# When later batches' loads are released, what runs in the head, and who copies the values: a change to a sketched-attention and routed-experts kernel

## The chip, the core and the metric

The kernel runs on one core of a Trainium2 chip. The core has five engines that run their own instruction streams: TensorE (PE; its weight loads are listed as PEld), VectorE (DVE), ScalarE (ACT), GpSimd (POOL) and SyncE (SP), which here only issues transfers. Transfers run on 16 DMA engines that all queues share. The metric is the device time of one execution in microseconds; less is better.

## The reference

The first half is an attention with a polynomial sketch in place of the softmax, on 4 batches, 4 heads, 1088 tokens and a head width of 32. The second sends each of the 4352 tokens, now 128 wide, to two of eight experts.

```python
def phi(x):
    a = np.einsum('rd,bhsd->bhsr', S1, x)          # r = 8
    b = np.einsum('rd,bhsd->bhsr', S2, x)
    return np.einsum('bhsi,bhsj->bhsij', a, b).reshape(*x.shape[:-1], r * r)
q_p, k_p = (phi(q), phi(k))
kv = np.einsum('bhsf,bhsd->bhfd', k_p, v)
z = np.sum(k_p, axis=2)
num = np.einsum('bhsf,bhfd->bhsd', q_p, kv)
den = np.einsum('bhsf,bhf->bhs', q_p, z)[..., None] + 1e-06
x = (num / den), heads side by side               # 4352 x 128
...
noisy_logits = x @ w_gate + np.log1p(np.exp(x @ w_noise)) * noise
top2 = the two largest of each row; top2_w = their softmax
for e in range(8):                                # w1[e]: 128 x 1024, w2[e]: 1024 x 128
    h = np.maximum(x[mask] @ w1[e], 0.0)
    out[mask] += top2_w[mask, k, None] * (h @ w2[e])
```

## The kernel before, in words

**The work.** For each batch, `keys_values` (L635) turns keys and queries by 32x32 blocks on DVE (`turned`, L581), and `features` (L591) makes the sketch of up to four tiles of 128 tokens: PE multiplies by the sketch matrix (L602), `lo` is copied out of PSUM, DVE adds (`ab`, L610) and forms the products (L624, `phk` for keys and `phq` for queries). PE then multiplies products of keys with `vaug`, a copy of the values (L661). `queries` (L698) transposes query products on PE (L709), multiplies (L720) and lets DVE divide. `router` computes gates, picks two experts, and counts on PE where each token goes (`mk`, L926 and L929). GpSimd scatters the weighted token rows to a table in HBM, `xs`, by indirect transfers (L801), each after a memset of `zb` that spaces them (L800).

**Waves and blocks.** The tokens come in five waves: wave 0 is four tiles of batch 0, wave 1 the rest of batch 0, waves 2 to 4 the batches 1 to 3. A `block` (L1022) is 128 or 256 rows of one expert: `xb` is fetched from `xs`, turned into `bT`, multiplied by `w1s` into `hp` (L1087), rectified into `h` (L1095, ACT), multiplied by `w2s` into `acc` (L1102), copied to `y`, and scattered to `pairs`, from which the output is summed. Blocks are counted from 0: 0 to 7 are wave 0's, 8 to 15 wave 1's, 16 to 23 wave 2's, and so on. Blocks 0 to 3 (`DIRECT`) don't go through HBM: PE gathers their rows with a selection matrix `o` made at L1032 (for block 0 two of its four parts on POOL, two on DVE). Blocks 4 to 7 (`QUICK`) are fetched by POOL, all later ones by SP, with four transfers for the rows and one for the indices, and are turned on DVE (L1077). `xb` has five buffers and `bT` three.

**What sets the order.** The order of the instructions on each engine is fixed when the program is built. `Plan` (L38) keeps for each job its engine (or a choice of engines), an estimated cost, a priority, and what it depends on, and takes at each step, of the jobs that could start within 0.3 us of the earliest, the one with the lowest priority number. `LAND`, `KLATE`, `VLATE`, `QLATE` and `MARGIN` are what the planner adds to a transfer's estimated arrival. The estimates only set the order; on the chip each instruction waits for the data it needs, in the order of its engine. `idle` (L1391) fills gaps of PE in the first 28 us with multiplications of zeros (L1407).

**Around the change.** `hold` keeps DVE and PE jobs of batch 1 behind the first router's choice. `later` marks transfers that wait until the fetches of blocks 4 to 7 are complete ("rows first"): the weights of experts 6 and 7, the clears of `xs` from row 512 up, and all loads of batches 2 and 3. All of them are issued by SP (L335), in the order of the plan. `kq` (keys and queries) has two buffers and `vld` (values) one.

Of the kernel before, what the change touches and what calls it, by code (L numbers as in the profile page):

```python
# [174 lines left out]
def kernel(  # L175
# [27 lines left out]
    C = 8  # L203
# [107 lines left out]
    MARGIN = 6.0  # L311
# [6 lines left out]
    def copy(e, o, i):  # L318
        paces.append(A.copy(o, i) if e == "ACT" else V.tensor_copy(o, i))  # L319

    held, hold_dma = [], [False]

    def later(*loads):
        hold_dma[0] = True
        for load in loads:
            load()
        hold_dma[0] = False

    def dma(q, o, i, r, w, prio, size=0, issue=0.45, after=(), done=None, margin=0.0):

        eng = {"SP": Y, "ACT": A, "POOL": G}
        waits = hold_dma[0]

        def emit(e):
            ins = eng[e].dma_start(o(), i())  # L335
            if waits:
                behind(ins, "rows first")
            if done:
                done(ins)
        job = add(q, issue, emit, r=r, w=w, prio=prio, lat=LAND, after=after, size=size)  # L340
        if hold_dma[0]:
            held.append(job)
        job.margin = margin
        return job
# [7 lines left out]
    def load_kq(b, which, prio):  # L352
# [4 lines left out]
                  margin=MARGIN if b > 1 or b and which == "q" else QLATE if which == "q" else KLATE)  # L357
# [223 lines left out]
    def turned(dst, src, c0, c1, prio):  # L581
# [7 lines left out]
        add("DVE", vec(128 * (c1 - c0) if c0 < C else 64), emit, r=[src], w=[(dst, t) for t in range(c0, c1)], prio=prio)  # L589

    def features(jobs, prio, after=(), first=None, early=None):  # L591
# [7 lines left out]
        def emit(e):  # L599
# [12 lines left out]
            in0=x4()[:, :, 0, :], in1=lo.t[rows, 0:n, :], op=ALU.add), r=[ps, lo], w=[ab], prio=prio)  # L612
# [19 lines left out]
    kv_of, behind_first = {}, []  # L632
    behind_gates = []

    def keys_values(b, prio, head=False, after=()):  # L635
        kT, qT, pk, pq, va = new("kT"), new("qT"), new("phk"), new("phq"), new("vaug")
        kld, qld, vld = klds[b], qlds[b], vlds[b]
        for h in range(H):
            add(EV if head else "ACT", either(256) if head else act(256), lambda e, h=h: copy(e, va.t[:, 0:C, h, 0:DH], vld.t[:, h, 0:C, :]),
                r=["ones_v"] + [(vld, l) for l in range(4)], w=[(va, h)], prio=prio + 2.2, after=hold)  # L640
        add("ACT", act(128), lambda e: A.copy(va.t[0:HB, C, :, 0:DH], vld.t[0:HB, :, C, :]),
            r=["ones_v", (vld, 4), (vld, 5)], w=[(va, H)], prio=prio + 2.2, after=hold)
        for i, (c0, c1) in enumerate(((0, 2), (2, 6), (6, 8)) if head else ((0, 4), (4, 8))):
            turned(kT, kld, c0, c1, prio + i)
            features([(kT, t, pk) for t in range(c0, c1)], prio + i + 1, after)
        turned(kT, kld, 8, 9, prio + 1)
# [375 lines left out]
    def block(u, w, e, r, n):  # L1022
# [5 lines left out]
        if u < DIRECT:  # L1028
            oh = new("o")
            for c in range(4):  # L1030
                add(("POOL" if u == 0 and c % 2 else "DVE"), 0.3 if u == 0 and c % 2 else vec(64), lambda e_, c=c: (
# [3 lines left out]
                    r=["place", onehot["pos"], onehot["gm"]], w=[(oh, c)], prio=-900 if u == 0 else 12 + u)  # L1035
# [8 lines left out]
        else:  # L1044
            xb, ix = new("xb"), new("ix")

            def done(ins):
# [3 lines left out]
                wrote(ins, "fetch")  # L1051
            there = routed.get(w, []) + routed.get(w - 1, [])
            rows = xs_e[e, r:r + P * n, :]
            if u < QUICK:
                def done(ins, done=done):
                    done(ins)
                    wrote(ins, "rows first")
                fetch = dma("POOL", lambda: xb.t[:, 0:n, :], lambda: rows.rearrange("(c p) x -> p c x", p=P),
                            there, [xb], -10 + u, size=66e3 * n, issue=0.55, done=done)
                for job in held:  # L1060
# [6 lines left out]
            else:  # L1067
# [3 lines left out]
                for l in range(4):  # L1071
                    dma("SP", lambda l=l: flat()[32 * l:32 * l + 32, :].rearrange("p (g x) -> p g x", x=32),
                        lambda l=l: rows[:, 32 * l:32 * l + 32].rearrange("(g p) x -> p g x", p=32),
                        there, [(xb, l)], -10 + u, size=16e3 * n, issue=0.5, done=done)
                dma("SP", lambda: ix.t[:, 0:n].unsqueeze(2), lambda: rows[:, D:XW].rearrange("(c p) x -> p c x", p=P),
# [269 lines left out]
    load_w(0, 41)  # L1345
    for r in (0, P):
        clear(r, 43)
    load_w(1, 44)
    for e in range(2, E - 2):
        load_w(e, 46 + e)  # L1350
    for r in (2 * P, 3 * P):
# [3 lines left out]
    later(lambda: load_w(E - 2, 53), lambda: load_w(E - 1, 54))  # L1355
    for r in range(4 * P, STATIC, P):
        later(lambda r=r: clear(r, 60 + r / P))
# [4 lines left out]
    keys_values(1, 100)  # L1362
    rest_of_queries(last)
    x, lg, last = queries(0, 4, C + 1, 27)
    router(0, 4, C + 1 - 4, 1, x, lg, 30)
    for b in range(1, B):
        if b > 1:
            later(lambda: load_kq(b, "k", 80 + 100 * b), lambda: load_kq(b, "q", 81 + 100 * b), lambda: load_v(b, 82 + 100 * b))
# [78 lines left out]
```

## Time and profile before

| | us |
|---|---|
| Median of 6 runs | 355.48 |
| Lowest and highest | 353.24 and 356.6 |
| The profiled execution's own time | 353.76 |
| Its span in the trace | 351.8 |
| PE, busy | 338.9 (96%) |
| PE, weight loads | 315.0 (90%) |
| POOL, busy | 233.3 (66%) |
| DVE, busy | 145.7 (41%) |
| ACT, busy | 134.4 (38%) |
| Fillers L1407, 33 of them | 11.1 |

Times in the trace count from the start of the span. A line of the page or of a view names an engine, a line of the code, and the tile that is written and those that are read; the mean duration is that of one instruction; "idle before" is how long the engine had nothing to run, with the instruction that ended the wait. The chain of waits goes back from the last instruction to whatever released it. A transfer appears with the instruction that issues it; when it has landed is seen from what it releases. Instruction records on PE are pipelined, so neighbours overlap by about 0.2 us.

The trace has these stages: until 27.43 the head (loads, batch 0, the first router); until 73.96 blocks 0 to 6 beside batch 1; then block 8 and after beside batches 2 and 3, until about 162; then blocks alone.

### The profile page before, as it was taken

The numbers are of one execution on the slowest core, as the hardware profiler recorded it, in microseconds if no ns is written. First come the engines' busy times: TensorE is split into PE (matmuls) and PEld (weight loads), VectorE is DVE, ScalarE is ACT, GpSimd is POOL, SyncE is SP. The second block draws the span as 40 slices with busy tenths as digits, with TensorE's granted clock in tenths as the row PEclk, the third lists the DMA queues.
The fourth block names the chain that finished last, engine by engine and source line by source line (L and its number), as shares of the span: only waits on it lengthen the run. The fifth ranks groups of instructions, "written<-read, shape, count | busy, mean of one in ns | idle before, by whom it ended". The sixth has DMA issues, their size and how long they took to land.

```text
span 351.8 us, 7486 instructions
## 1 busy us (share of the span) xinstructions
PE 338.9 (96%) x2589; PEld 315.0 (90%) x2590; DVE 145.7 (41%) x547; ACT 134.4 (38%) x301; POOL 233.3 (66%) x385
## 2 busy tenths in 40 slices
PE   8999999969999999999999999999999999999992
PEld 3859999969999999998999999999999999999991
DVE  5879893847966887586301000011012000001401
ACT  2343532534325333333333433343334333434330
POOL 7758569962898989988898988954433443344510
PEclk9999999999999999999999999999999999999997
DMA  8999859933351135512422223553215311115521
GB/s 207 323 345 248 297 141 358 315 70 81 72 169 47 41 69 89 135 47 45 86 60 61 50 48 71 129 156 52 46 31 145 100 39 23 29 25 147 162 81 38
DMA packets 68298, 41.17 MB, mean 117 GB/s; under 512 B 49301, under 2 KB 60438, under 8 KB 68256
## 3 DMA queue, kind: packets, MB, share of 16 engines
q1 hardware_dynamic: 62784, 30.92, 35.4%
q0 software_dynamic: 4736, 9.19, 7.9%
q10 hardware_dynamic: 736, 0.54, 0.6%
q8 instruction: 21, 0.34, 0.4%
q14 instruction: 21, 0.17, 0.2%
HBM read 24.17 MB, written 16.65 MB: 116 GB/s over the span
## 4 chain that ended last, share of the span: by engine, by line
PE 84%; POOL 6%; DVE 5%; DMA 2%; issue 2%; ACT 1%; SPq 0%; POOLq 0%; DVEq 0%
PE acc L1102 33%; PE hp L1087 33%; PE bank L602 4%; POOL xs L801 3%; PE bank L720 3%; PE bank L661 2%; PE bank L709 2%; PE hp L1407 2%; POOL zb L800 1%; PE acc L661 1%; DMA pairs<-y,first_at 1%; PE turn L1038 1%; PE bank L1234 1%; DVE pick L904 1%; DMA xb<-xs 1%
## 5 line engine op out<-in xcount | busy, mean ns | idle before, releaser
L1087 PE MATMUL hp<-bT,w1s 128*128 128x128 f32 (+1 forms) x768 | 148.6, 329 | 3.0 <-DVE bT L1077 3.0
L1102 PEld LDWEIGHTS acc<-w2s,h 128*128 128x128 f32 x1152 | 146.7, 192 | 4.8
L1102 PE MATMUL acc<-w2s,h 128*128 128x128 f32 x1152 | 150.7, 275 | 0.0
L1095 ACT ACTIVATE h<-hp 128x512 f32<-128x512 f32 x144 | 86.0, 597 | 131.8 <-PE hp L1087 131.8
L1087 PEld LDWEIGHTS hp<-bT,w1s 128*128 128x128 f32 x768 | 111.6, 192 | 8.7 <-issue 3.4
L801 POOL DMA_INDIRECT pairs<-y,ix x62 | 62.1, 1002 | 66.1 <-ACT y L319 59.1
L801 POOL DMA_INDIRECT xs<-xg,to x72 | 72.5, 1007 | 13.6 <-issue 9.3
L1077 DVE STREAM_TRANSPOSE bT<-xb 128x256 f32<-128x256 f32 (+1 forms) x40 | 15.5, 388 | 131.6 <-PE hp L1087 124.0
L800 POOL MEMSET zb<- 128x400 bf16 (+1 forms) x142 | 62.8, 443 | 0.2
L319 ACT COPY y<-acc 128x128 f32<-128x128 f32 (+1 forms) x48 | 15.3, 319 | 26.3 <-PE acc L1102 26.3
L1158 DVE TENSOR_TENSOR o<-pr 128x512 f32<-128x512 f32 (+2 forms) x13 | 6.7, 522 | 30.4 <-DMA pr<-pairs 30.4
L720 PE MATMUL bank<-kvw,pT 128*128 128x98 f32 x144 | 18.7, 274 | 0.0
L720 PEld LDWEIGHTS bank<-kvw,pT 128*128 128x128 f32 x144 | 17.5, 192 | 0.7 <-DVE kvw L319 0.3
L319 ACT COPY pT<-bank 128x512 f32<-128x512 f32 (+1 forms) x19 | 10.2, 540 | 8.1 <-PE bank L709 7.3
L661 PE MATMUL bank<-phk,vaug 128*128 128x128 f32 (+1 forms) x108 | 13.1, 278 | 0.0
L661 PEld LDWEIGHTS bank<-phk,vaug 128*128 128x128 f32 (+1 forms) x108 | 12.6, 191 | 0.4
L1407 PE MATMUL hp<-zb 128*128 128x512 bf16 x33 | 11.1, 464 | 1.7 <-DVE zb L436 1.3
L319 ACT COPY lo<-bank 128x256 f32<-128x256 f32 (+3 forms) x20 | 6.5, 331 | 15.8 <-PE bank L602 14.8
L624 DVE TENSOR_TENSOR phk<-ab 128x512 f32<-128x512 f32 (+1 forms) x20 | 12.3, 628 | 0.4
L624 DVE TENSOR_TENSOR phq<-ab 128x512 f32<-128x512 f32 (+1 forms) x20 | 12.1, 636 | 0.3
L978 DVE TENSOR_TENSOR xg<-x,g 128x512 f32<-128x512 f32 (+1 forms) x16 | 11.3, 751 | 0.0
L709 PE MATMUL bank<-ident,phq 128*128 128x128 f32 x72 | 11.3, 279 | 0.0
(175 smaller groups left out, 242.6 us busy)
## 6 DMA issues: line engine op xcount, KB each, us to landing
xs<-pad SPq DMA_DIRECT2D x9, 516.0 KB
w1s<-in_moe_w_dram SPq DMA_DIRECT2D x8, 512.0 KB
w2s<-in_moe_w_dram SPq DMA_DIRECT2D x8, 512.0 KB
pr<-pairs SPq DMA_DIRECT2D x7, 512.0 KB
xb<-xs SPq DMA_DIRECT2D x96, 32.0 KB
kq<-in_k_dram SPq DMA_DIRECT2D x4, 544.0 KB
kq<-in_q_dram SPq DMA_DIRECT2D x4, 544.0 KB
vld<-in_v_dram SPq DMA_DIRECT2D x14, 128.0 KB
```

Of the source, the lines that this page charges most:

```text
L319: paces.append(A.copy(o, i) if e == "ACT" else V.tensor_copy(o, i))
L624: V.tensor_tensor(out=jobs[i][2].t[rows, jobs[i][1]:jobs[m - 1][1] + 1, :, :].rearrange("p c h (i j) -> p (c h) i j", i=R), in0=factors(i, ...
L661: T.matmul(kvp.t[:, P * a:P * a + P], lhsT=va.t[0:K, t, hs, :].rearrange("p h d -> p (h d)"), rhs=pk.t[0:K, t, hs, :].rearrange("p h f -> ...
L709: T.transpose(ps.t[:, c0:c0 + P], pq.t[:, t + i, 2 * a:2 * a + 2, :].rearrange("p h f -> p (h f)"), ident[:])
L720: T.matmul(ps2.t[:, c0:c0 + 2 * YW], lhsT=pT.t[:, P * (2 * i + a):P * (2 * i + a) + P], rhs=kvw.t[:, a, :], start=True, stop=True)
L800: G.memset(zb[:, 0:FIRST_SPACER if kind == "first" else SPACER], 0.0)
L801: ins = G.indirect_dma_start(**kw)
L1077: add("DVE", vec(P * n), lambda _: V.transpose(bT.t[:, 0:P * n], flat()), r=[xb], w=[bT], prio=TOP + u)
L1087: T.matmul(hp.t[:, P * n * i:P * n * (i + 1)], lhsT=w1s[:, e, P * (js * g + i):P * (js * g + i + 1)], rhs=bT.t[:, 0:P * n], start=True, st ...
L1095: paces.append(A.activation(out=h.t[:], in_=hp.t[:], func=AF.Relu))
L1102: T.matmul(acc.t[:, D * c:D * c + D], lhsT=h.t[:, P * (n * i + c):P * (n * i + c + 1)], rhs=w2s[:, e, j, :], start=(j == 0 and c == 0), st ...
L1407: ins = T.matmul(warm()[:], lhsT=zb[:, 0:P], rhs=zb[:], start=True, stop=True)
```

## The change

- `later` takes the number of a block. The weights of experts 6 and 7 and the clears still wait for the fetches of blocks 4 to 7. The loads of batch 2 now wait for the fetch of block 8, those of batch 3 for the fetch of block 16.
- The planner's `MARGIN` for the loads of batches 2 and 3 goes from 6 to 3 us; that of batch 1's queries stays 6.
- Everything in the plan from the first clear and expert 1's weights up to expert 5's is put behind batch 0's key transposes (`freed`), and so behind batch 1's keys.
- The first four key tiles of batch 1 are transposed without regard to `hold`, and their sketch is run on PE as soon as the last query tile of the first router has been multiplied, into an `acc` buffer. Their products stay where they were. The rest of batch 0's queries, which go the same way, are now listed ahead of batch 1.
- The adds (L610) of these two early sketches get priorities 12.95 and 13.2, ahead of the selection matrices of blocks 1 to 3, which go from 12 + u to 12.5 + u.
- In the head the four value copies may go to ACT or POOL, where they could go to ACT or DVE.
- Of block 0's selection matrix one part of four is made on POOL, not two; its estimated cost there is 0.85, not 0.3.

```diff
-    MARGIN = 6.0
+    MARGIN = 3.0
...
     def copy(e, o, i):
-        paces.append(A.copy(o, i) if e == "ACT" else V.tensor_copy(o, i))
+        if e == "POOL":
+            G.tensor_copy(o, i)
+        else:
+            paces.append(A.copy(o, i) if e == "ACT" else V.tensor_copy(o, i))
...
-    def later(*loads):
-        hold_dma[0] = True
+    def later(u, *loads):
+        hold_dma[0] = u
...
-            if waits:
-                behind(ins, "rows first")
+            if waits is not None:
+                behind(ins, "rows %d" % waits)
...
-                  margin=MARGIN if b > 1 or b and which == "q" else QLATE if which == "q" else KLATE)
+                  margin=MARGIN if b > 1 else 6.0 if b and which == "q" else QLATE if which == "q" else KLATE)
...
-            in0=x4()[:, :, 0, :], in1=lo.t[rows, 0:n, :], op=ALU.add), r=[ps, lo], w=[ab], prio=prio)
+            in0=x4()[:, :, 0, :], in1=lo.t[rows, 0:n, :], op=ALU.add), r=[ps, lo], w=[ab], prio=prio if early is None else 12.95 if jobs[0][2] is kv_of[0][1] else 13.2)
...
-            add(EV if head else "ACT", either(256) if head else act(256), lambda e, h=h: copy(e, va.t[:, 0:C, h, 0:DH], vld.t[:, h, 0:C, :]),
+            add(("ACT", "POOL") if head else "ACT", {"ACT": act(256), "POOL": 0.4} if head else act(256), lambda e, h=h: copy(e, va.t[:, 0:C, h, 0:DH], vld.t[:, h, 0:C, :]),
...
-            turned(kT, kld, c0, c1, prio + i)
+            if early is not None and i == 0:
+                turned(kT, kld, c0, c1, 22, True)
+                features([(kT, t, pk) for t in range(c0, c1)], prio + i + 1, after, 21.5, early)
+                continue
+            freed.append(turned(kT, kld, c0, c1, prio + i))
...
-                add(("POOL" if u == 0 and c % 2 else "DVE"), 0.3 if u == 0 and c % 2 else vec(64), lambda e_, c=c: (
+                add(("POOL" if u == 0 and c == 3 else "DVE"), 0.85 if u == 0 and c == 3 else vec(64), lambda e_, c=c: (
...
-                    r=["place", onehot["pos"], onehot["gm"]], w=[(oh, c)], prio=-900 if u == 0 else 12 + u)
+                    r=["place", onehot["pos"], onehot["gm"]], w=[(oh, c)], prio=-900 if u == 0 else 12.5 + u)
...
-                wrote(ins, "fetch")
+                wrote(ins, "fetch", "rows %d" % (u if u >= QUICK else DIRECT))
...
+                    for job in held.get(u, ()):
+                        job.deps.add(fetch)
...
+    first_loads = len(plan.jobs)
     for r in (0, P):
         clear(r, 43)
     load_w(1, 44)
     for e in range(2, E - 2):
         load_w(e, 46 + e)
+    for job in plan.jobs[first_loads:]:
+        job.deps.update(freed)
...
-    later(lambda: load_w(E - 2, 53), lambda: load_w(E - 1, 54))
+    later(DIRECT, lambda: load_w(E - 2, 53), lambda: load_w(E - 1, 54))
...
-    keys_values(1, 100)
     rest_of_queries(last)
+    keys_values(1, 100, early=last)
...
-            later(lambda: load_kq(b, "k", 80 + 100 * b), lambda: load_kq(b, "q", 81 + 100 * b), lambda: load_v(b, 82 + 100 * b))
+            later(8 * b - 8, lambda: load_kq(b, "k", 80 + 100 * b), lambda: load_kq(b, "q", 81 + 100 * b), lambda: load_v(b, 82 + 100 * b))
```

## The prediction

> **What bounds the kernel now.** I read the page's chain first, then who waited on TensorE (PE), then the chain in order of time around the longest wait, then the timelines of GpSimd (POOL) and the load queue (SPq). Blocks are counted from 0, so the "ninth block" is block 8, the "seventeenth" block 16.
>
> The page's chain that ended last, and the PE waits from 60 to 200 us (columns: total us, times, longest):
>
> ```profile
> PE 84%; POOL 6%; DVE 5%; DMA 2%; issue 2%; ACT 1%; SPq 0%; POOLq 0%; DVEq 0%
> ```
>
> ```profile
> PE hp L1087 <- DVE bT L1077: 3.0, 1, 3.0
> PE bank L926 <- DVE mk L919: 1.1, 2, 0.6
> ```
>
> PE is the bound, and its granted clock is 1.00 in all but the last stretch. From the first block on it waits for one transpose (3.04 us) and twice for a router's mask (0.51 and 0.61). So only three things can shorten the run: those waits, an earlier first block, and real work put where the head runs filler matmuls (L1407). The long wait, in the chain in order of time (start, us, what):
>
> ```profile
> 67.67 0.90 POOL xs L801
> 68.57 0.45 POOL zb L800
> ...
> 69.19 4.08 DMA pairs<-y,first_at
> 73.27 0.28 SPq L335
> ...
> 74.54 1.93 DMA xb<-xs
> ...
> 76.55 0.32 DVE bT L1077
> 76.88 0.14 issue
> 77.01 1.13 PE hp L1087 x8
> ```
>
> Block 8 is fetched from rows that wave 1 scatters. The last of ten scatters ends its issue at 68.57; the fetch leaves only at 73.23, 4.66 us later. The chain names the result scatter beside it, but the timeline of POOL shows a copy (L971) let go at 73.23 by `xs<-xg,to`, so I take the row scatter as what was late. PE is idle from 73.96 to 77.01, with work of blocks 6 and 7 queued behind the waiting matmul. What the DMA engines did (start:end, length, busy us of the engines, PE clock, DMA share, GB/s):
>
> ```profile
> 60.00:64.00 4.00, 4.00 (x42) 3.83 (x41) 2.68 (x6) 2.43 (x8) 3.66 (x6) 1.00 1.04 357
> ...
> 66.00:68.00 2.00, 2.00 (x20) 1.97 (x19) 1.53 (x7) 0.79 (x2) 1.69 (x3) 1.00 1.00 385
> ...
> 70.00:72.00 2.00, 2.00 (x20) 2.00 (x19) 1.51 (x7) 0.00 (x0) 1.62 (x3) 1.00 0.63 174
> 72.00:74.00 2.00, 1.97 (x18) 1.73 (x16) 0.32 (x1) 0.97 (x3) 0.56 (x3) 1.00 0.13 41
> ```
>
> They are full until about 71. SPq had issued weights 6 and 7 and five clears from 48.35, then batch 2's keys, queries and values (8 issues, 1.67 MB) from 56.58 to 67.41. The same step in wave 2, from the timelines of POOL and SPq:
>
> ```profile
> 118.59 0.90 POOL L801 DMA_INDIRECT xs<-xg,to  x1 [0.17 <-issue]
> ```
>
> ```profile
> 120.75 1.35 SPq L335 DMA_DIRECT2D xb<-xs  x3
> ```
>
> The last scatter's issue ends at 119.49 and the fetch leaves 1.26 us later; in wave 3 it is 161.62 to 163.64, 2.02 us.
>
> **The sum, part by part** (against the profiled execution's 353.76 us: span 351.8 and 1.96 around it).
>
> 1. **Batch 2's loads held until block 8's fetch.** 1.67 MB at 385 GB/s is 4.3 us of full DMA, so the rest drains at about 67, before the last scatter is issued. The fetch then leaves 1.26 to 2.02 us after 68.57, which is 2.6 to 3.4 earlier; the wait of 3.04 becomes 0 to 0.4. Taken: **-2.8**. Bounds: -3.04 (all) and 0 (the queue, not the loads, is slow). The two row scatters of other waves are the nearest rows, so I stay near the upper gain.
>
> The Trainium skill, "DMA: Bandwidth & Descriptors", section "Queues, rings and completion order", says that each DMA engine goes round the queues that have work, a packet at a time; a small scatter in a queue of its own would then share, not stand in line. By it a 66 KB scatter at half of 385 GB/s loses some 0.2 us (an estimate), step 1 is worth 0.2, and the sum would be -1.4. The 4.66 against 1.26 says otherwise.
>
> 2. **First block's selection matrix.** It is made by four instructions of L1032, two on POOL at 0.83 each and two on DVE at 0.28:
>
> ```profile
> 25.72 1.66 POOL L1032 TENSOR_SCALAR o<-place,pos,gm 128x128 f32<-128x128 f32 x2 [0.81 <-DVE pos L947]
> ```
>
> ```profile
> 26.14 1.78 PE L1038 MATMUL turn<-o,x 128*128 128x128 f32 x8 [0.30 <-DVE o L1032]
> ```
>
> The last gather matmuls wait for POOL's second, done at 27.39. With one on POOL (25.72 to 26.55) and three on DVE (25.65 to 26.49) they go 0.84 earlier, and block 0 with them: **-0.84**. Bounds: -0.84 and 0 (if ScalarE's second copy of a sketch, 0.36, holds up bT; the row has it idle 2.2 us there).
>
> 3. **Part of batch 1's key sketch in the head.** The first four key tiles, 8 matmuls, run at 37.70 for 0.90; PE runs 17 fillers from 20.45 to 25.27. Moved there they cost nothing: **-0.9**. Their transpose (0.65) needs DVE idle time, which is 1.30 and 1.22 us before 18.62, and the keys by then. Their load is now issued at 11.53 behind weights 1 and a clear (1.6 MB, about 4 us at 385 GB/s); the change puts it ahead. Bounds: -0.9, and +0.65 if the transpose sits in the router's chain.
>
> 4. **Value copies.** Four at 0.40 on ScalarE end at 10.29 and hold the first value matmuls at 10.16. GpSimd's nearest row, the noise copy of 256 elements, takes 0.39, and it has 1.52 us idle at 8.58; two copies there end the set some 0.5 earlier. DVE's products feed the rest, so little comes through: **-0.3**, bounds -0.9 (the eight matmuls' 0.94 all filling a gap) and +0.8 (two copies that POOL does late).
>
> The Trainium skill, "SBUF — State Buffer", section "Who interferes with whom", has GpSimd and a DVE instruction with two SBUF inputs exclude each other. The products L624 are such; by it two copies could hold DVE 0.8 us (an estimate) and the sum would be 1.1 worse. L624 takes 0.65 to 0.69 with POOL busy or idle in this trace; a 256-element POOL copy beside it is not shown.
>
> 5. **DVE's new order after the gate.** The third matrix instruction (0.28) and two adds (0.41 each) now stand ahead of block 1's matrix, 1.1 us. Now it ends at 30.10 and the gather starts at 30.16, so nothing covers it but block 0's second half, 1.79, which PE can run first when the accumulators are free (that is what the early adds give). Taken **+0.4**, bounds 0 and +1.1. Wave 0's scatters shift by 0.7 behind these; fetches of blocks 4 to 7 have 2 us in hand (47.3 landed, by 44.43 + 0.55 + 2.3; used at 49.76).
>
> 6. **Wave 2's router.** DVE sat idle 4.23 us before block 8's transpose with batch 1's router queued behind it, and then ran batch 2's transposes (1.30), add (0.39) and product (0.69) inside it. These go later. The mask's wait of 0.51 shrinks: **-0.4**, bounds -0.51 and 0.
>
> 7. **What is late next.** From 77.01 to 130.60 PE used 3.4 us of batch 3's sketches as cover before block 16. They now wait behind block 16's fetch. Steps 1 to 6 (4.8 us) and this bring PE to block 16 at 130.6 - 4.8 - 3.4 = 122.4; its transpose ended at 127.5. But the router that feeds it starts 2.8 earlier and loses 2.4 of foreign work, so the fetch leaves near 115.6 instead of 120.75, and the transpose, 4.4 later at best (1.9 issue, 1.9 landing, 0.44), is done near 120: 2 us in hand. Batch 2's eight loads stand behind up to 25 fetch issues of 0.44 (11 us, with five buffers), land about 88, and its chain from transposes to values needs some 12 us of DVE; blocks 6 to 15 give PE 34 us meanwhile. A new mask wait like those of 0.5 to 0.6 and some slip: **+0.8**, bounds 0 and +3.7 (below).
>
> Sum: -2.8 - 0.84 - 0.9 - 0.3 + 0.4 - 0.4 + 0.8 = **-4.0**; 353.76 becomes 349.7. The median shown, 355.48, is 1.7 above the profiled execution, so as a median I say **351.4**.
>
> **Rivals.** (0.5%, 1.8 us, is about what a measurement of this kernel can tell from no change; faster is below 353.7, slower above 357.3.)
> - *All covers hold:* the copies give 0.9, block 1 costs nothing, no wait comes in: -5.9, 349.6. For: the idle rows are there. Against: seven orders at once.
> - *The loads are not what holds the scatter:* step 1 gives nothing: -1.2, 354.3, no change. For: the chain names the result scatter of 69.19. Against: waves 2 and 3, where results follow too.
> - *The early sketch doesn't get its keys:* the transpose waits within the router's chain: step 3 turns from -0.9 to +0.65, 353.0, or 354 where later copies go with it.
> - *Block 16 becomes the wait (slower):* it decides from where block 16's transpose ends after 130.6 - 3.4 = 127.2, as the 3.4 us of sketches come after it. As late as now (127.5) this is +0.3; with the batch 2 loads lying on wave 2's scatters as they now lie on wave 1's (4.66 - 1.26 = 3.4 later) it is +3.7, 359.2. For: no batch 3 work is left as cover. Against: the loads are some 20 us ahead of the last scatter.
>
> **How the numbers follow.** Forecast 0.55; all covers hold 0.16; loads not the cause 0.12; no early keys 0.06; block 16 waits 0.11. Faster: 0.55 + 0.16 and half of the keys' case, 0.74; same 0.15; slower 0.11. Range 349.0 to 356.5: it leaves out the slower case and some of the best.
>
> **What would show it.** Right: the fetch of block 8 within 2 us of the last wave 1 scatter and no PE wait near 72 to 75; one POOL L1032; eight L602 before the gate in place of fillers; SPq's batch 2 loads after block 8's fetches. Wrong: a PE wait before the first block of wave 2 (L1087 with 128x256), a scatter that still lands 4 us late with the loads gone, or gaps between 28 and 36 while DVE makes block 1's matrix.

## The result, and the profile after

| | before | after |
|---|---|---|
| Median, us | 354.92 (81 runs) | 353.93 (39 runs) |
| Ratio to before | | 0.9966 [0.9952, 0.9981] |
| Profiled execution, own time | 353.76 | 352.30 |
| Its span | 351.8 | 350.6 |
| PE's last matmul starts | 345.36 | 343.65 |
| Fillers (L1407, now L1417) | 33, 11.1 us | 29, 9.9 us |

The change takes 0.34% off, about 1.2 us, where 4.0 were forecast. Ratios, here and below, leave out executions in a slow state (over 1.5% above the fastest of the same kernel) while medians are of all, so the two need not agree. Lines have moved: L1087 is now L1094, L1077 is L1084, L1032 is L1040, L1038 is L1046, L602 is L606, L801 is L809, L335 is L338, L971 is L979.

The page's chain that ended last, after:

```profile
PE 85%; SPq 4%; DVE 4%; DMA 3%; issue 1%; POOL 0%; ACT 0%; DVEq 0%; POOLq 0%
```

POOL's scatters (6% before) have left the chain; SP's queue (0% before) has come into it. PE's waits from 60 to 200 us (total us, times, longest):

```profile
PE hp L1094 <- DVE row L965: 0.9, 1, 0.9
PE hp L1094 <- ACT h L1102: 0.7, 1, 0.7
PE bank L934 <- DVE mk L927: 0.6, 1, 0.6
PE bank L606 <- DVE kT L590: 0.5, 1, 0.5
PE bank L606 <- issue: 0.3, 1, 0.3
```

The wait of 3.0 us for block 8 is gone. Five small ones stand in its place, and together they are as long: 0.9 at 82.4 us, 0.3 at 88.3, 0.6 at 129.5, 0.5 at 146.3, 0.7 at 154.5.

The step that was to go first went as forecast. POOL's last scatter of wave 1, and SP's queue after it (start, length, what):

```profile
66.10 0.90 POOL L809 DMA_INDIRECT xs<-xg,to  x1 [0.17 <-issue]
```

```profile
68.39 1.76 SPq L338 DMA_DIRECT2D xb<-xs  x4
70.19 2.37 SPq L338 DMA_DIRECT2D ix<-xs  x5
72.73 0.33 SPq L338 DMA_DIRECT2D kq<-in_k_dram  x1
73.10 0.43 SPq L338 DMA_DIRECT2D kq<-in_q_dram  x1
73.58 0.43 SPq L338 DMA_DIRECT2D vld<-in_v_dram  x1
77.31 6.93 SPq L338 DMA_DIRECT2D xb<-xs  x12
...
140.82 0.59 SPq L338 DMA_DIRECT2D kq<-in_k_dram  x1
```

The scatter's issue ends at 67.00 and block 8's fetch leaves 1.39 us later (4.66 before). Read on, though: after three of batch 2's loads SP stands still from 74.01 to 77.31. The next instruction fetches block 9 (the expectations below call it block 10) into a sixth `xb`, and there are five; blocks 4 to 7 give theirs back only when their result scatter has landed. SP's queue waits, from 60 to 100 us:

```profile
SPq L338 <- DMA pairs<-y,xb: 3.2, 1, 3.2
```

The chain in order of time that follows (start, us, what):

```profile
78.16 0.43 SPq L338
...
78.65 3.14 DMA xb<-xs
...
81.91 0.31 DVE bT L1084
...
82.37 1.13 PE hp L1094 x8
```

The last of block 9's four transfers took 3.14 us (block 8's took 1.93 in the trace of before). DVE stands idle 4.34 us ahead of 81.91 with the rest of batch 1's router queued behind the transpose, and PE waits 0.92.

The last line of SP's queue above is batch 3's keys, at 140.82: the hold lets them go at 115.8, but block 16's fetches and those behind it, paced by the five buffers, come first. DVE, from 120 to 180 us, waits for them:

```profile
DVE kT L590 <- DMA kq<-in_k_dram: 7.2, 1, 7.2
```

The keys land at 145.48, and the PE waits of 146 to 155 us follow from it (keys, their values, the products). In the trace of before all of batch 3's keys were sketched by 121.

In the head, the gate's result is ready at 24.90 (25.42 before), the early sketch runs at 19.68 in place of fillers, and the first block starts at 27.61 (28.28 before). Block 0's selection matrix on DVE, and the gather that reads it on PE:

```profile
25.13 1.30 DVE L1040 TENSOR_SCALAR o<-place,pos,gm 128x128 f32<-128x128 f32 x3
```

```profile
26.58 0.68 PE L1046 MATMUL turn<-o,x 128*128 128x128 f32 x4 [0.18 <-DVE row L965]
```

Three instructions take 1.30 us. The first two take 0.35 and 0.39 with starts 0.26 apart, as before (0.66 for the two there); the third, 0.72.

### The profile page after: what moved, and what is told of

Same layout as the page of the kernel before. It is cut to its first block, busy times and chain, and to the rows that moved or that the text cites. A ratio compares the mean times of both kernels' runs of the same rounds, so it can differ in the third digit from the quotient of the medians.

```text
span 350.6 us, 7473 instructions
## 1 busy us (share of the span) xinstructions
PE 338.0 (96%) x2585; PEld 314.5 (90%) x2586; DVE 146.3 (42%) x550; ACT 132.6 (38%) x297; POOL 233.4 (67%) x386
## 4 chain that ended last, share of the span: by engine, by line
PE 85%; SPq 4%; DVE 4%; DMA 3%; issue 1%; POOL 0%; ACT 0%; DVEq 0%; POOLq 0%
PE hp L1094 32%; PE acc L1109 32%; PE bank L606 5%; PE bank L728 4%; SPq L338 4%; PE bank L669 4%; PE bank L717 2%; PE hp L1417 2%; DMA xb<-xs 1%; DMA kq<-in_k_dram 1%; PE acc L669 1%; PE turn L1046 1%; PE bank L1241 1%; DMA pairs<-y,ix 1%; DVE xg L986 1%
## 5 line engine op out<-in xcount | busy, mean ns | idle before, releaser
L1109 PEld LDWEIGHTS acc<-w2s,h 128*128 128x128 f32 x1152 | 146.3, 192 | 5.2 <-issue 0.2
L1094 PE MATMUL hp<-bT,w1s 128*128 128x128 f32 (+1 forms) x768 | 148.5, 329 | 1.6 <-DVE row L965 0.9
L1094 PEld LDWEIGHTS hp<-bT,w1s 128*128 128x128 f32 x768 | 111.6, 191 | 7.8 <-issue 1.4
L809 POOL DMA_INDIRECT pairs<-y,ix x62 | 60.8, 980 | 59.3 <-ACT y L322 49.3
L809 POOL DMA_INDIRECT xs<-xg,to x72 | 73.9, 1026 | 25.2 <-DVE xg L986 12.0
L1084 DVE STREAM_TRANSPOSE bT<-xb 128x256 f32<-128x256 f32 (+1 forms) x40 | 15.5, 389 | 119.8 <-PE hp L1094 112.6
L322 ACT COPY pT<-bank 128x512 f32<-128x512 f32 (+1 forms) x17 | 9.2, 548 | 12.3 <-PE bank L717 12.2
L1417 PE MATMUL hp<-zb 128*128 128x512 bf16 x29 | 9.9, 475 | 1.6 <-DVE zb L439 1.3
L986 DVE TENSOR_TENSOR xg<-x,g 128x512 f32<-128x512 f32 (+1 forms) x16 | 11.1, 748 | 0.0
```

What stands on the lines that cost most here:

```text
L809: ins = G.indirect_dma_start(**kw)
L1094: T.matmul(hp.t[:, P * n * i:P * n * (i + 1)], lhsT=w1s[:, e, P * (js * g + i):P * (js * g + i + 1)], rhs=bT.t[:, 0:P * n], start=True, st ...
L1109: T.matmul(acc.t[:, D * c:D * c + D], lhsT=h.t[:, P * (n * i + c):P * (n * i + c + 1)], rhs=w2s[:, e, j, :], start=(j == 0 and c == 0), st ...
L1417: ins = T.matmul(warm()[:], lhsT=zb[:, 0:P], rhs=zb[:], start=True, stop=True)
```

## The experiments

Kernels sent together ran on one chip, in one job, with runs of the kernel before among them. Ratios go to these; pairs of one job are the sharpest. The changed kernel's own 0.9966 comes from none of these jobs, so a comparison with it is rough. "Rows" stands for seven row buffers in place of five (with eight `y` for the room).

| job | run | median us | ratio to before |
|---|---|---|---|
| 1 | hold alone | 353.95 | 0.9997 [0.9967, 1.0026] |
| 1 | the rest without hold, margin 6 | 355.31 | 1.0009 [0.9974, 1.0043] |
| 1 | after, margin 6 | 351.84 | 0.9928 [0.9896, 0.9961] |
| 1 | after, batch 3 at block 8 | 350.26 | 0.9880 [0.9836, 0.9923] |
| 2 | after, rows | 350.15 | 0.9853 [0.9818, 0.9888] |
| 2 | after, old selection matrix | 353.35 | 0.9956 [0.9932, 0.9980] |
| 2 | after, no early sketch | 354.87 | 0.9973 [0.9942, 1.0004] |
| 2 | after, margin 6 and batch 3 at block 8 | 353.47 | 0.9961 [0.9931, 0.9992] |
| 3 | after, margin 6, batch 3 at block 8, rows | 348.56 | 0.9818 [0.9771, 0.9865] |
| 3 | after, margin 6, rows | 348.78 | 0.9825 [0.9776, 0.9875] |
| 3 | hold alone, rows | 349.52 | 0.9842 [0.9795, 0.9889] |
| 3 | before, twelve fillers | 357.31 | 1.0066 [1.0032, 1.0100] |
| 4 | before, rows | 353.19 | 0.9952 [0.9929, 0.9975] |
| 4 | before, 24 fillers | 357.13 | 1.0064 [1.0042, 1.0086] |
| 4 | after, eight `y` only | 353.77 | 0.9980 [0.9952, 1.0008] |
| 4 | after, old value copies | 356.10 | 1.0016 [0.9977, 1.0054] |
| 5 | before, eleven fillers | 355.71 | 1.0016 [0.9990, 1.0041] |
| 5 | the rest without hold, margin 6, rows | 356.02 | 1.0033 [1.0012, 1.0054] |

### Does the hold do what step 1 says?

```diff
 the rest without hold, margin 6 (against the changed kernel):
-    MARGIN = 3.0
+    MARGIN = 6.0
...
-            later(8 * b - 8, lambda: load_kq(b, "k", 80 + 100 * b), ...
+            later(DIRECT, lambda: load_kq(b, "k", 80 + 100 * b), ...
 margin 6 (against the changed kernel): the first of these edits alone
 hold alone: before with the second line as the changed kernel has it, and what it needs
```

> The kernel before with one part of the change alone: batch 2's loads wait for block 8's fetch and batch 3's for block 16's; margin 6, head and first matrix as before. Step 1 of the prediction: the 3.04 us wait goes and nothing comes back but the 0.8 of step 7, so the time falls by some 2 to 2.8 us (ratio to before 0.992 to 0.994). Theory A (given back): the fetch of block 8 leaves within 2 us of the last wave 1 scatter and the wait is gone, but late loads of batches 2 and 3 bring back most of it: -1 to +0.5 us (0.997 to 1.001). Rival B (the loads did not hold the scatter): the fetch still leaves 4 us or more after the scatter.

> The changed kernel without its hold: loads of batches 2 and 3 wait for the first rows only, as before, and the margin is 6 again; the head's three edits stay. Theory A: -1.5 us (0.66 from an earlier first block, 0.9 from the sketch), ratio 0.995 to 0.997, as good as the whole change, with a wait of some 3 us before block 8 as before. If the hold were worth what step 1 says, this kernel would be some 2 us slower than the whole change (ratio 1.000 to 1.003).

The rest without the hold and the changed kernel with margin 6 differ in the hold alone, and ran in one job: 1.0009 against 0.9928, 0.8% or 2.9 us for the hold, by the two intervals some 1 to 4.5. Step 1 had 2.8. POOL in the kernel without the hold (last scatter, then the copy that its landing lets go), and SP's first fetch:

```profile
66.49 0.91 POOL L809 DMA_INDIRECT xs<-xg,to  x1 [0.17 <-issue]
73.15 0.22 POOL L979 COPY xg<-pid 128x18 int32<-128x18 int32 x1 [2.54 <-DMA xs<-xg,to]
```

```profile
73.15 1.73 SPq L338 DMA_DIRECT2D xb<-xs  x4
```

The same scatter and fetch with the hold:

```profile
66.52 0.91 POOL L809 DMA_INDIRECT xs<-xg,to  x1 [0.17 <-issue]
```

```profile
68.82 1.76 SPq L338 DMA_DIRECT2D xb<-xs  x4
```

Scatters at the same time; the fetch leaves at 73.15 without the hold and at 68.82 with it, 5.75 and 1.39 us after the scatter's issue. The rival that the loads do not hold the scatter falls. What was wrong was my own expectation that the rest alone would be worth 1.5 us. Its first block starts 0.9 us earlier than before's and its scatters end 1.2 us earlier, but the fetch still leaves at 73: PE waits 4.5 us there in place of 3.0. The late fetch takes up what PE gains ahead of it, and in this plan more than that. The chain in order of time at the end of the wait (start, us, what):

```profile
74.46 3.13 DMA xb<-xs
...
77.67 0.06 DVE bT L1084
...
80.14 0.60 DVE h L1100
80.78 2.07 PE hp L1094 x8
```

Block 8's transpose is done at 77.98, but PE goes on only at 80.78: it needs the rectification of block 7's hidden layer (L1100), which stands on DVE behind that transpose and behind the router that follows it. Behind the wait the clock is halved for 6.8 us (below). So the 2.9 us between the two kernels hold more than the queue's lateness, and that they agree with step 1's 2.8 is partly luck; the fetch times are the cleaner evidence.

The wait takes up what PE loses ahead of it, too, and this is the likely reason for the result of the hold alone (no trace of the kernel before was taken in its job). Its 0.9997 is the ratio that Theory A expected, but not for Theory A's reason. Its fetch left 1.40 us after the scatter's issue, and PE had no wait before block 8. But its trace has PE idle near 37 to 43 us, longest here:

```profile
PE bank L606 <- ACT pT L322: 1.4, 1, 1.4
```

Between the starts of blocks 1 and 4 it loses 3.0 us against the usual pace of its matmuls (the sum of the gaps between starts above the common gap of the same matmul), where before's trace loses 0.6 with the same order of instructions on every engine to that point. Four traces of that order show this stall (hold alone, before with rows, before with 24 and with eleven fillers) and three do not (before, before with twelve fillers, hold alone with rows); they go by job, so the chip may have a part in it. With the stall PE comes to block 8 at 77.06 and 77.56 (the two filler runs) and finds its transpose all but done: 77.70 and 76.73. The wait of 3.0 hides the stall. Take the wait away and the stall should count. What the stall is, I could not settle: ACT and DVE start late on work whose inputs were ready. No trace of the changed head has it.

### What gave it back: margin, hold of batch 3, row buffers

```diff
 batch 3 at block 8:
-            later(8 * b - 8, lambda: load_kq(b, "k", 80 + 100 * b), ...
+            later(8, lambda: load_kq(b, "k", 80 + 100 * b), ...
 rows:
-    tag("xb", 5, [P, 2, XW])
-    tag("ix", 5, [P, 2])
-    tag("y", 10, [P, 2 * D])
+    tag("xb", 7, [P, 2, XW])
+    tag("ix", 7, [P, 2])
+    tag("y", 8, [P, 2 * D])
```

> The changed kernel with the planner's margin for loads of batches 2 and 3 at 6 us again, in place of 3. Theory A1 (the margin is what gives it back: the plan puts batch 3's transposes and matmuls where its loads have not landed): DVE's 7.16 us wait for batch 3's keys goes or halves, the PE waits of 146 to 155 us (0.49, 0.2, 0.7 to 0.85) go, 1 to 1.5 us less than the changed kernel, ratio to before 0.992 to 0.994. Rival A2 (the hold at block 16 is what gives it back, whatever the plan): within 0.5 us of the changed kernel, 0.995 to 0.998.

> The changed kernel with batch 3's loads let go after block 8's fetch too, like batch 2's; margin 3. Theory A2: batch 3's keys land before 140 us, its sketch stands ahead of the block it is now behind, the PE waits of 146 to 155 us go, 1.5 to 2 us less than the changed kernel, ratio 0.990 to 0.993. Rival: batch 3's loads, once free, lie beside wave 2's scatters as batch 2's did beside wave 1's, and block 16 waits for its rows: a new PE wait of 1 us or more near 120 us, no gain (0.996 or more).

Both have lower ratios than the changed kernel's 0.9966 (with margin 6 the intervals overlap), and both traces lose the waits of 146 to 155 us. So both theories of the cause after block 16 fit: they are two handles on one thing, batch 3's keys arriving after the plan uses them. With margin 6 PE's waits from 60 to 200 us are:

```profile
PE hp L1094 <- DVE row L965: 0.8, 1, 0.8
PE bank L606 <- DVE lim L998: 0.8, 1, 0.8
PE bank L690 <- ACT pT L322: 0.2, 1, 0.2
```

The three of 146 to 155 us are gone, though batch 3's keys still leave SP at 140.80: the plan now has blocks there. DVE's wait for them:

```profile
DVE kT L590 <- DMA kq<-in_k_dram: 1.5, 1, 1.5
```

1.5 in place of 7.2. From block 16 to the end PE loses 3.7 us to gaps, as before, and 5.8 in the changed kernel. Released at block 8, batch 3's keys leave at 97.48 and PE loses 3.2 there.

> The changed kernel with seven row buffers (xb, ix) in place of five, and eight result buffers (y) in place of ten to make the room. Theory C (the load queue is held by the rows' buffers: block 10's fetch waits 3.2 us for result scatters, then shares the DMA engines with batch 2's loads; DVE stands still 4.3 us behind it and PE 0.92): the wait near 82 us goes, batch 2's router runs earlier, 0.9 to 1.5 us less than the changed kernel, ratio to before 0.992 to 0.994. Rival: batch 2's loads now stand behind more fetches, its keys come later, and PE waits near 88 us for as long: 0.996 to 0.998.

> The changed kernel with eight result buffers in place of ten, row buffers five as they are: the control for the runs with seven row buffers. All theories: as the changed kernel, 0.995 to 0.998; if it came out near 0.985, the y buffers and not the row buffers would be what those runs changed.

Rows alone give 0.9853, and 0.9853 against 0.9956 for the changed kernel but for its selection matrix, in the same job, is 1.0%, some 3.5 us. (The ratios to before are flattered in this job: the mean granted clock was below 0.993 in 27 of 29 executions of the kernel before, in the job of the hold alone in 10 of 29. The pair is not.) Eight `y` alone give 0.998: the row buffers do it. PE's waits with rows, from 60 to 200 us:

```profile
PE bank L606 <- DVE qT L588: 1.4, 1, 1.4
PE bank L606 <- DVE kT L590: 0.7, 1, 0.7
PE bank L606 <- DVE ab L614: 0.5, 1, 0.5
```

The wait at 82 us is gone, as the theory of the row buffers had it, and in this execution (353.05, the slowest of the six) its rival had a part too: batch 2's keys now leave after more fetches, at 88.77 in place of 72.73, and PE waits for them near 98 us. The gain was above both expectations, and where it comes from is not shown: the trace with the old selection matrix, the partner of the pair, has no wait at 82 us either. The clock (below) may have a part.

> The kernel before with seven row buffers (eight y) and nothing else: loads of batches 2 and 3 still go with the first rows. Theory C (hold and buffers need each other: the hold frees block 8's fetch, the buffers free block 10's): the wait of 3 us before block 8 stays and the run gains little, 0.995 to 1.001, against 0.984 with the hold. Rival F (the buffers are the whole gain, the hold is worth nothing): 0.984 to 0.988.

> The changed kernel with margin 6 and seven row buffers but without the hold (all loads of batches 2 and 3 go with the first rows). Theory C with the head's gain taken up by the wait before block 8 (the rows of wave 1 come when GpSimd and the DMA queues are done, not when PE is): 0.993 to 0.997, about the kernel before with seven buffers (0.995), and a wait of 3 us or more before block 8. Rival (the head's edits alone need the buffers, as the hold did): 0.985 or less.

> The kernel before with the hold alone (margin 6, as in the first run of this study) and seven row buffers (eight y). Theory C: the hold's 2.8 us of step 1 were there, but block 10's fetch, held by the row buffers and then run beside batch 2's loads, gave them back; with seven buffers the hold alone gives 2 to 3 us, ratio 0.991 to 0.994. Rival (the head's edits are needed to turn the hold into time): as the hold alone, 0.998 to 1.001.

Rows without the hold: 0.9952 on the kernel before, 1.0033 on the changed one. With the hold: 0.9842 and 0.9825. So the buffers are not the whole gain; with them the hold is worth some 1 to 2% (different jobs, so roughly). For the pair on the kernel before I expected the hold to need the buffers. Rows and hold together do give it, but the hold alone (0.9997) is no fair partner, since its trace has the stall of 2.5 us and this one's does not. Nor is the kernel before with rows: its trace has the stall as well, and no wait before block 8, where I had expected one of 3 us. One pair is fair: hold, margin 6 and rows with the head before and with the changed head, 0.9842 and 0.9825 in one job. All the edits in the head together are worth 0.2% there, 0.6 us, which the intervals can't tell from nothing.

The changed kernel with rows and without the hold shows best what late rows do. PE's longest wait from 27 to 200 us, and its windows there (start:end, length, busy us of PE, PEld, DVE, ACT, POOL, PE's granted clock, DMA share, GB/s):

```profile
PE hp L1094 <- ACT h L1102: 5.5, 1, 5.5
```

```profile
78.00:80.00 2.00, 0.00 (x0) 0.00 (x0) 0.94 (x10) 0.00 (x0) 1.83 (x3) 1.00 0.41 85
80.00:82.00 2.00, 0.00 (x0) 0.00 (x0) 0.57 (x6) 0.10 (x1) 0.55 (x1) 1.00 0.23 51
82.00:84.00 2.00, 1.36 (x6) 1.36 (x7) 1.12 (x16) 1.37 (x4) 0.27 (x1) 0.54 0.18 24
84.00:86.00 2.00, 2.00 (x13) 2.00 (x12) 1.87 (x7) 1.19 (x4) 0.57 (x2) 0.60 0.26 31
86.00:88.00 2.00, 2.00 (x27) 1.99 (x27) 1.00 (x5) 0.47 (x3) 0.43 (x1) 1.00 0.26 32
```

The last scatter's issue ends at 67.79, the fetch leaves at 74.05, 6.26 us later; and the wait is followed by 3.4 us at half the clock. Block 8's transpose is done at 77.62. What ends the wait comes later (chain, start, us, what):

```profile
77.77 3.54 DMA xb<-xs
...
81.43 0.31 DVE bT L1084
...
81.89 0.21 ACT g L906
82.11 0.49 ACT h L1102
```

That is block 9's fetch. DVE stands at its transpose with the router behind it, ACT waits for the router's next step (L906) with the rectification behind it, and PE waits for that.

> The changed kernel with both mends: margin 6, and batch 3's loads let go after block 8's fetch. If margin and hold are two causes, their gains add: 0.984 to 0.986 (about -5 us against before). Theory A (one cause: batch 3's loads land later than the plan puts their first use; either mend removes it): no better than the earlier release alone, 0.987 to 0.989.

> The changed kernel with margin 6 and seven row buffers, batch 3's loads held as the change has them. Theory A1 with C: the PE waits of 97 to 99 us (batch 2's keys) and 147 to 150 us (batch 3's) that the kernel with seven buffers had go, as the plan puts their use later: 0.980 to 0.985. Rival: no better than seven buffers alone, 0.985 to 0.988.

> The changed kernel with all three mends: margin 6, batch 3's loads let go after block 8's fetch, seven row buffers (eight y). Theory C (the row buffers' wait near 82 us, 0.92 to 2.0 us from one execution to the next, is what undid the other mends when both were in): the wait at 82 us is gone, little is left after block 16, and the median is at or below that of the seven buffers alone: ratio 0.980 to 0.986. Rival (batch 3's loads, let go early, take TensorE's cover away elsewhere): 0.988 or more.

Both mends without rows do not add up: 0.9961, above either, and I expected at worst 0.989. From block 16 to the end its trace loses only 2.8 us, so both did their work; it lost 4.3 near 78 to 89 us, where the changed kernel's trace lost 1.8. The wait at 82 us was 1.8 in place of 0.92, and the clock fell behind it. That wait differs from trace to trace (0.8 with margin 6, 1.0 with the old value copies, 1.2 with batch 3 at block 8, none with the old selection matrix), and this job's chip is not that of the two mends, so their 0.9928 and 0.988 may be partly luck of place. All three mends together have the lowest ratio here, 0.9818, 1.8% (5.9 us between the medians) below before; with margin 6 and rows the hold on batch 3 costs nothing that can be measured (0.9825).

I expected the wait for block 9's rows to go with seven buffers. In two of the traces with the hold it doesn't. With all three mends PE waits 0.9 us at 77.5 us. With margin 6 and rows it waits 2.7 at 79.1, in an execution of 352.27 us, the slowest of six with a median of 348.78:

```profile
PE hp L1094 <- ACT h L1102: 2.7, 1, 2.7
```

Block 9's fetch leaves right behind block 8's there, and batch 2's keys only at 90.39, but the fetch's last transfer still takes 3.58 us, and DVE, ACT and PE stand behind it as above. So the buffers decide when the fetch leaves, and they are not all that decides when its rows are there.

### What a wait of PE costs: the clock

The windows above show it; so does the trace of both mends without rows, at its 1.8 us wait:

```profile
82.00:84.00 2.00, 0.15 (x2) 0.10 (x1) 0.50 (x3) 0.00 (x0) 0.41 (x1) 1.00 0.37 67
84.00:86.00 2.00, 2.00 (x14) 2.00 (x14) 1.59 (x7) 0.60 (x1) 0.00 (x0) 0.71 0.23 34
86.00:88.00 2.00, 2.00 (x11) 2.00 (x11) 2.00 (x4) 0.27 (x1) 0.61 (x1) 0.50 0.48 118
88.00:90.00 2.00, 2.00 (x19) 2.00 (x19) 1.93 (x8) 0.60 (x1) 1.83 (x3) 0.93 0.58 154
```

A clock of 0.71, 0.50 and 0.93 is 1.16, 2.00 and 0.28 us at half: 3.4 in all, 1.7 us of matmuls lost, as much as the wait itself. The Trainium skill, "TensorE: Matmul & The Clock Gate", section "Part 1: The HAM clock gate (the "warmup" mystery)", says that the clock is halved by windows of some 3.4 us that run on their own, after an idle one. The length agrees with the 3.4 here. Its section "Why this matters for your kernels" warns of gaps over about 3 us; here 1.8 us was enough, while the 3.04 us of before's trace had no dip behind it. The mean clock of an execution tells of such dips: of all the traces, nine have one before the last stretch and mean clocks of 0.983 to 0.992, the other eleven 0.993 to 0.997. To see whether this is part of before's time I filled that wait.

```diff
+                if u == 8 and g == 0:
+                    for _ in range(12):
+                        T.matmul(hp.t[:], lhsT=zb[:, 0:P], rhs=zb[:], start=True, stop=True)
 second and third form: 24 and 11 times
+                        T.matmul(hp.t[:, 0:P], lhsT=ident[:], rhs=ident[:], start=True, stop=True)
```

> The kernel before with twelve filler matmuls (0.22 us each, into the bank that block 8's first matmul overwrites) ahead of block 8's first matmul, so that PE runs them while it waits there; nothing else is changed and no work is saved. Theory E (a wait of 2 us or more sometimes halves the granted clock for about 3.4 us behind it, and each such dip costs 1.7 us; the executions differ by the number of dips): the clock is 1.00 behind the wait in every execution, mean clocks lie at 0.993 or more, and the median falls by 0.5 to 1.5 us (ratio 0.996 to 0.998). Rival (the wait alone counts): 0.999 to 1.001, with clocks spread as before.

> The kernel before with 24 filler matmuls of the identity by itself (0.11 us each, 2.65 us) ahead of block 8's first matmul, in place of the fillers that were held by a write of their operand. They depend on nothing that is late, so PE runs them inside the wait. Theory E (the wait sometimes halves the granted clock for 3.4 us or twice that, 1.7 us lost each time): the clock is 1.00 behind the wait in nearly every execution, and the median falls by 0.5 to 1.5 us, 0.996 to 0.999. Rival (the wait alone counts): 0.999 to 1.002.

> The kernel before with eleven filler matmuls of the identity ahead of block 8's first matmul: the run with 24 showed that each is two passes of 0.11 us, so that its fillers lasted 5.3 us and outlasted the wait; eleven last 2.4 us. Theory E (the clock that falls behind the wait costs time besides the wait): mean clocks at 0.993 or more in nearly all executions, median 0.5 to 1 us lower, ratio 0.997 to 0.999. Rival (the wait alone counts, and where PE arrives late the fillers cost up to 2.4 us): 1.000 to 1.004.

None of the three settles it. In the first the fillers read a tile that POOL writes, so the first of them waited as long as block 8 would have, and all ran behind the wait at half the clock:

```profile
77.23 5.30 PE L1088 MATMUL hp<-zb 128*128 128x512 bf16 x12 [3.54 <-POOL zb L800]
```

Twelve in 5.30 us are 0.44 each, twice the 0.22 of the head. In the second each identity matmul was two passes, 5.5 us in all. In the third they lasted 2.6 us, but PE came to them at 77.56 (the stall), when there was no wait to fill: 1.0016, less than their price. The mean clock was 0.993 or more in 21 of the 24 executions of the second and third form, and in 40 of 57 of the kernel before in the same two jobs; that points the way of the theory and is no proof of a gain. The executions of the kernel before say more. In each of the five jobs those with a mean clock of 0.993 or more have the lower median: 354.4 against 355.1 us, 354.7 (two executions) against 355.6, 353.5 against 355.3, 354.4 against 355.1, 354.8 against 355.0. So a fallen clock goes with 0.2 to 1.7 us more; where in the run it fell is not shown. What stands besides is what the traces show: half clock for 3.4 us (seven traces) or 6.8 us (two), behind single gaps of 1.8 to 5.5 us, behind two of 1.4 and 0.5 and, in the stall, behind one of 1.2; and none behind 3.04 in before's trace, 1.9 and 1.4 in two others, or 0.92 in that of the changed kernel. It may be why taking away the wait at 82 us gave more than its own 0.92.

### The head's parts

> The changed kernel with block 0's selection matrix made as before by two instructions on GpSimd and two on DVE (the plan is told 0.85 us for each on GpSimd, so that it expects them where they are). Step 2 of the prediction: the first block starts 0.84 us later and the run is as much longer (ratio 0.998 to 1.000). Theory D (step 2 was worth 0.14, since DVE's own three slow down beside GpSimd's one: 0.35, 0.39 and 0.72 in place of 0.28 each): the first block starts 0.1 to 0.3 us later, the DVE instructions near 25 us take less time each, and the run is the same as the changed kernel's (0.996 to 0.998).

> The changed kernel without the early sketch: batch 1's first four key tiles are transposed and sketched after the gate as before, its keys are loaded in their old place, and the adds have their old places. Step 3 of the prediction: PE has 0.9 us more to do behind the first block, ratio 0.999 (0.9 us above the changed kernel's 0.9966), if nothing covers it; block 1's new wait of 0.36 us stays if it comes from the third matrix instruction and goes if it comes from the adds. Rival: the wave 1 scatters, not PE, set the start of block 8, and the 0.9 us is lost in the wait before it: ratio as the changed kernel's, 0.996 to 0.997.

> The changed kernel with the value copies as before (ScalarE and DVE in place of ScalarE and GpSimd). Step 4 of the prediction: 0.3 us slower, the first block 0.3 us later. What the trace says: the gate's result is 0.52 us later again and with it the first block, ratio 0.998 (0.5 us above the changed kernel). Rival: no difference.

```diff
 old selection matrix:
-                add(("POOL" if u == 0 and c == 3 else "DVE"), 0.85 if u == 0 and c == 3 else vec(64), ...
+                add(("POOL" if u == 0 and c % 2 else "DVE"), 0.85 if u == 0 and c % 2 else vec(64), ...
 no early sketch (and neither freed nor the early priorities of the adds):
+    keys_values(1, 100)
     rest_of_queries(last)
-    keys_values(1, 100, early=last)
 old value copies:
-            add(("ACT", "POOL") if head else "ACT", {"ACT": act(256), "POOL": 0.4} if head else act(256), ...
+            add(EV if head else "ACT", either(256) if head else act(256), ...
```

With the old selection matrix the gate's result is ready at 24.89 (24.90 in the changed kernel) and the first block starts at 27.75 (27.61): the edit is worth 0.14, and the whole run is as fast (0.9956). The gather's last two passes there:

```profile
26.91 0.49 PE L1046 MATMUL turn<-o,x 128*128 128x128 f32 x2
```

POOL's second is ready at 26.86. In the changed kernel DVE's third is ready at 26.43, 0.43 earlier, but four passes are still to come, not two. And block 1 starts 4.69 us behind block 0 with the old matrix, 5.48 with the new. My guess that DVE's instructions would each be shorter with two of them on POOL was half right: the two take 0.35 and 0.39 in both; only the third, 0.72, is gone.

Without the early sketch: 0.9973 against 0.9956 for the kernel with the old selection matrix in the same job, 0.6 us of the 0.9, with intervals that overlap. The 0.6 is no measure of the sketch, as this plan has another wait: PE stands 2.3 us before the mask of wave 2's router (85.2 us), with the clock halved for 3.4 us behind it. Block 1 starts 4.63 us behind block 0 there, and the wait of 0.36 is gone, as it is with the old matrix. With the old value copies the gate is 0.45 later (25.35) and the first block 0.46 (28.07), which agrees with the trace; the ratio, 1.0016, is too wide to add to that.

## Why the prediction was wrong, step by step

The sum of what the two traces show, against the -1.46 between the two profiled executions (-1.2 by the ratio): block 8's wait -3.04, first block -0.14 for the matrix and -0.52 for the copies, sketch -0.9, block 1's wait +0.36, block 9's 0.92 in place of the mask's 0.51, batch 2's keys +0.34, masks 0.59 in place of 0.61, batch 3 +1.38 (0.49, 0.2, 0.69), and 0.5 more between the last matmul and the end: -1.6.

1. *Batch 2's loads held:* right in mechanism, and in size by the traces (2.8 forecast, 3.04 gone). The experiments say less on the size: 2.9 with the changed head, partly by luck, and nothing for the hold alone. The rule of the Trainium skill, "DMA: Bandwidth & Descriptors", section "Queues, rings and completion order", by which the scatter would lose 0.2 us, does not cover it: 5.75 and 6.26 us to the fetch against 1.39.
2. *Selection matrix:* failed. "One on POOL and three on DVE, 0.84 earlier" was 0.14, since DVE's third took 0.72 and not 0.28, and two more passes stand behind the last part. The 0.28 was also misread: it is the pace of block 1's four, and block 0's own two took 0.66 in before's trace.
3. *Early sketch:* right in mechanism. It got its keys (transposed at 17.10) and ran in place of fillers, and the rival without keys falls; its 0.9 us in the whole run is not shown by itself.
4. *Value copies:* better than forecast, 0.52 for 0.3, and inside its bounds.
5. *DVE's order:* right, 0.36 for 0.4. It goes with the old matrix and also without the early sketch, so it takes both the third instruction and the two adds.
6. *Wave 2's router:* failed. The mask's 0.51 went, but the router stood 4.34 us behind block 9's transpose, and 0.92 came in.
7. *What is late next:* failed in size, and it is the step that decides, with step 2 behind it. Block 16 was as forecast (fetch at 115.82 for 115.6, transposed at 120 for 120), so the slower rival was rightly held unlikely. But 0.8 was 2.6: 0.92 at block 9, 0.34 for the transposes of batch 2's keys, which DVE ran behind the late router, 1.38 after batch 3's keys, and a mask of 0.59 where before's trace had one of 0.61. Two things were missed. The five buffers were counted as issue time, not as a wait that stops the queue in the middle of batch 2's loads. And the planner's margin, 6 to 3, was listed among the edits and priced nowhere; with it set back, the waits of 1.38 go, and the ratio is 0.4% lower, though between jobs and with intervals that overlap.

The rival "the loads are not what holds the scatter" had nearly the right time for the wrong reason. The sum also added the head's gains to step 1 without saying that they hang on it: without the hold the same head edits are worth nothing (1.0009), since the wait at block 8 takes them. The 0.5 us at the end of the run was in no step, and its cause is open.

## What to carry to other kernels

A wait that a queue ends can take up the gains and losses ahead of it: work out what ends it before adding gains in front of it, and what stands behind the late data on the other engines. When loads are held back, follow each queue past the point of release and ask which buffer count will stop it there, and who waits behind it; the buffer may be worth more than the hold. Price planner constants in a diff like any other edit, and count a TensorE wait of about 2 us as possibly twice its length.

## What the runs showed that I had not expected

- Half the granted clock for 3.4 us behind waits as short as 1.8 us (once 1.2), and for 6.8 us behind 3.5 and 4.5.
- A DVE instruction of 128x128 that takes 0.35 and 0.39 as first and second took 0.72 as third beside POOL's 0.87, in every trace of the new order, also in the one without the early adds. It ended 0.35 us after POOL's; the cause is open.
- The same order of instructions lost 2.4 to 3.4 us near 37 to 43 us in some jobs and nothing in others, while ACT and DVE had their inputs; the cause is open.
- A row fetch that landed in 1.93 us in before's trace took 3.14 in the changed kernel's, though the DMA engines moved only 41 and 18 GB/s from 79 to 81 us, and 3.54 and 3.58 in the runs with rows without the hold and with margin 6, where SP had no loads to issue beside it. My theory that batch 2's loads slow it is not borne out; the cause is open.
